# Order of the forward weave's steps, and of the work at the border behind it, in a fused attention forward and backward kernel

## The chip, the cores and the metric

The kernel runs on one core of a Trainium2 chip. The metric is the device time of one execution in microseconds (us); several executions are timed and their median is taken. The core has five engines: TensorE (PE; weight loads are shown as PEld), VectorE (DVE), ScalarE (ACT), GpSimd (POOL) and SyncE (SP, which issues DMA transfers). Each runs its own instructions in order and waits on semaphores for the others.

## The reference, cut to what matters

The reference computes two attention layers on the same 2048 tokens of width 576, mixes them with a gate, and takes all gradients.

```python
# A: 32 heads of width 18, one shared key and value (k = x @ wk, v = x @ wv)
scores = einsum('bhqd,bkd->bhqk', q, k) * 18 ** -0.5
a = merge(einsum('bhqk,bkd->bhqd', softmax(scores), v)) @ wo
# B: 32 heads of width 128, segments of 32 tokens, 8 memory rows carried from one to the next
for s in range(64):
    h = concat([mem, x[32 * s:32 * s + 32]])          # 40 rows
    q, k, v = (einsum('btd,dhe->bhte', h, W) for W in (Wq, Wk, Wv))
    p = softmax(where(mask, einsum('bhqe,bhke->bhqk', q, k) * 128 ** -0.5, -1e9))
    o = einsum('bhte,hed->btd', einsum('bhqk,bhke->bhqe', p, v), Wo)
    mem, out_s = o[:8], o[8:]
out = g * a + (1 - g) * b                              # g = sigmoid(x . gate_w)
# and the gradients of out with respect to x, every weight, mem0 and gate_w
```

Layer B's memory makes its segments a chain: segment s + 1 cannot begin before the eight memory rows of segment s are known. Layer A has no such chain.

## The kernel before, in words

The program runs in stages. First come transposes, weights and the projections of all tokens (to 420 us). Then the **forward weave** (420 to 2060): the forward chain of layer B's memory rows and the first sweep over layer A's pairs of query and key tiles, interleaved by hand. Then the **bulk** (2060 to 2660): layer B's attention and its gradients for all tokens of all segments at once. A second weave (2660 to 4335) joins the backward chain to a second sweep over layer A, and the weight gradients end the program.

**The weave.** `weave` (L277) advances two generators in turn, two sweep steps ahead: one part of the chain, then one step of the sweep. The order of the instructions on each engine is the order of these calls; no scheduler moves them.

- The chain, `b_chain_fwd` (L338), yields 16 times a segment, 64 segments. A sweep has 1024 steps, numbered n; the text calls n % 16 the **place**. The first part of a segment stands in front of place 2, the second in front of place 3, and so on.
- The parts that matter: part 1 (in front of place 2) takes `row_sums` (L306): four transposes of 32-bit values by PE into c_pj, summed by DVE into the new memory rows hm. Parts 2 to 4 project the keys: two halves ("k", 0) into c_pj and ("k", 1) into c_x, five contraction tiles each, four matmuls a tile (four column groups of the array, side by side). Before, parts 2, 3, 4 hold 2, 4 and 4 tiles (L461 to L472). Parts 5 to 7 project queries and the later ones values. In part 11 POOL normalises the probabilities (c_pn) and spreads them over heads by `expand` (L260): c_PBm for the memory rows, then c_PBx for the tokens (L520, L521). In part 13 (in front of place 14) PE multiplies tokens' values by c_PBx and then memory values by c_PBm (L531 to L535).
- The sweep, `a_pass1` (L1761): in step n, PE makes the scores a_S of tile n + 1 and a_dP of tile n; ACT takes the exp of a_S into a_E (L1778); DVE multiplies a_dP by a_E into a_W (L1811); PE then adds tile n - 1's a_E and a_W to a_acc. There is one a_S buffer. All 16 key tiles of a query block make one round of 16 steps; then ACT copies a_acc to a_acs (place 0) and a generator `a_post` (L1840) finishes the block in pieces: at place 3, ahead of the scores, two transposes of a_acs into c_x (the tile name that the chain's second key half also uses) and ACT's copy to a_tk; at place 10 two transposed loads of the queries a_qt; at place 14 two transposes into c_pj and DVE's copy to a_tk; at place 15 some fifteen small operations on POOL, with the results stored by SP.

**The border.** For the last query block all of `a_post` runs behind the last step, its small operations on DVE. Its a_qt takes a buffer of the a_W ring, so SP's two transposed loads wait until one is free; its a_tk is the one buffer that the block before it still reads on POOL. `b_bulk` (L664) then clears four block-diagonal tiles x_vmB and x_kmB on DVE (L669, L670, 128x1024 words each) and issues the loads of its first chunks on SP (L918 to L924). Every row of its loop over t runs a list of pipelined pieces, `order`, with their lags: t transposes queries and keys of group t (`trans`, L770, copied by DVE for q and k, by ACT for dO and v), takes scores and exp of group t - 1, and transposes dO and v of group t - 2. Four groups make a chunk. x_tr, which takes the transposes, has two buffers.

Which waits guard what is decided when the program is built: each instruction waits for the last reader or writer of the tile, or of the memory that a new tile takes over. Loads on SP also wait, in order, for the eighth load before them.

Of the kernel before, what the change touches and what calls it, by code (L numbers as in the profile page):

```python
# [12 lines left out]
BF16 = mybir.dt.bfloat16  # L13
F32 = mybir.dt.float32
U16 = mybir.dt.uint16
U32 = mybir.dt.uint32
P = 128

D = 576
# [27 lines left out]
class Kern:  # L47
# [290 lines left out]
    def b_chain_fwd(self, keep, sp, psum):  # L338
        nc = self.nc
        NSEG = self.NSEG  # L340
        hm = self.hm
        hx = keep.tile([P, 3, 64], F32, name="c_hx")
        PBm = keep.tile([P, 8, 64], BF16, name="c_PBm")
        nc.vector.memset(hx[:], 0.0)
# [63 lines left out]
        for s in range(NSEG):  # L408
# [49 lines left out]
            nc.gpsimd.tensor_copy(hist[:, :, s, :], h_[:, 0:NKT, 0:8])  # L458
            if not last:
                put_ride(s + 1)  # L460
            proj("k", 0, (0, 1))  # L461
            yield
            proj("k", 0, (2, 3, 4))
            proj("k", 1, (0,))
            if wt is not None:
                stash_end(*wt)
                wt = None
# [1 line left out]
                nc.gpsimd.dma_start(self.pq_dram[s // 4].rearrange("c i q s h x k -> (c i q) (s h x k)")  # L469
                                    .rearrange("p (n z) -> p n z", z=256), z4[:].unsqueeze(1).to_broadcast([P, 8, 256]))  # L470
            yield
            proj("k", 1, (1, 2, 3, 4))  # L472
            yield
            self.evac(flat(t2["k"], 1), pj["k", 1][:], use="s")
            proj("q", 0, (0, 1, 2, 3))
# [41 lines left out]
            pn = sp.tile([P, 2, 64], BF16, name="c_pn", bufs=1)  # L517
            nc.gpsimd.tensor_tensor(out=pn[:], in0=Et[:], in1=rd[:].unsqueeze(1).to_broadcast([P, 2, 64]), op=ALU.mult)
            PBx = sp.tile([P, 8, 4, 8], BF16, name="c_PBx", bufs=1)
            self.expand(PBm[:, :, 0:32].rearrange("p u (c q) -> p u c q", q=8), pn[:, 1].rearrange("p (u q) -> p u q", q=8), 8)  # L520
            self.expand(PBx[:], pn[:, 0].rearrange("p (u q) -> p u q", q=8), 8)  # L521
            nc.gpsimd.dma_start(self.pm_dram[s], pn[:].rearrange("p a b -> p (a b)"))
            proj("v", 1, (0, 1))
            yield
# [139 lines left out]
    def b_bulk(self, wp, vp, kp, sp, psum):  # L664
        nc = self.nc
        NTT = self.NTT
        mx = self.maskX
        mB = {w: [wp.tile([P, 4, 4, E], BF16, name=f"x_{w}mB{i}") for i in range(2)] for w in ("k", "v")}
        for t in mB["v"] + mB["k"]:  # L669
            nc.vector.memset(t[:], 0.0)  # L670
        mT = {}
        C = {}
        NG = NTT * 8
# [33 lines left out]
        deep = self.RING  # L707
# [62 lines left out]
        def trans(t, w, nb):  # L770
            tt, g, r, d = view(t)
            pt = psum.tile([P, 4, P], BF16, name="x_tr", bufs=2)
            for i in range(4):
                self.tr(pt[:, i, :], d[w][:, 4 * (g % 4) + i, :], P)
            o = sp.tile([P, 4, P], BF16, name=f"x_{w}T", bufs=nb)
            self.evac(o[:], pt[:], use="s" if w in ("dO", "v") else "v")
            sc[w + "T", t] = o

        st_QT = lambda t: trans(t, "q", 2)
# [135 lines left out]
                 (5, st_K), (3, st_D), (5, st_KE), (3, st_O), (5, st_Q)]  # L915
        after = {st_O: (("vB", 0), ("v", 0)), st_D: (("mT", 0),), st_KE: (("q", 0), ("dO", 1)), st_Q: (("kB", 0), ("k", 3))}
        later = {}
        load(0, ("q", "k", "mT", "dO"))  # L918
        load(1, deep)
        load(0, ("v", "vB", "kB"))  # L920
        load(1, ("v", "vB", "kB"))
        load(2, deep + ("mT", "v"))
        for c in range(3, BQ):
            load(c, deep)  # L924
        for t in range(NG + 6):
            if t == NG - 8:
                self.sweep_first()
            sc["D"] = psum.tile([P, 512], F32, name="x_D", bufs=1)
            sc["Sb"] = psum.tile([P, 512], F32, name="x_S", bufs=1)
            for n, st in order:  # L930
                if n is None:
                    st(t)
                    continue
                if 0 <= t - n < NG:
                    st(t - n)
                if st in after and t - n >= 0 and (t - n) % 4 == 3:
                    c = (t - n) // 4
                    for w, wait in after[st]:
                        later.setdefault(t + wait, []).append((c + (BQ if w in deep else 3 if w in ("mT", "v") else 2), (w,)))
                        if wait == 0:  # L940
                            load(*later[t].pop())
            if t % 4 == 2 and t // 4 - 2 in range(NTT // 4):
                self.dl_rows(t // 4 - 2, sp, psum)
            for x in later.pop(t, ()):
                load(*x)
            flush(t >= NG)
# [814 lines left out]
    def a_pass1(self, keep, sp, psum, xps):  # L1761
        nc = self.nc
        T, NTT = self.T, self.NTT
        NB = NPR * (T // 512)
        dl_all = self.dl_all
        S, E_, W_ = {}, {}, {}
        QD, load = self.QD, self.load_QD

        def mm_S(n):
            S[n] = psum.tile([P, 2, 512], F32, name="a_S", bufs=1)  # L1770
            kt = n % 16
            for i in range(2):
                r = slice(32 * i, 32 * i + 32)
                self.mm(S[n][:, i, :], lhsT=self.KV[r, kt * P:kt * P + P], rhs=QD[n // 16][r, :], tp=(32 * i, 0))

        def ex(n):
            E_[n] = sp.tile([P, 2, 512], BF16, name="a_E", bufs=3)
            nc.scalar.activation(E_[n][:], S.pop(n)[:], ACT.Exp, scale=SCALEA)  # L1778

        def acc_mm(acc, n, src, st, halves, first, last):  # L1780
            t = src.pop(n)
            for h in halves:
                for g in range(4):
                    self.mm(acc[32 * g:32 * g + 32, 256 * h:256 * h + 256],
                            lhsT=st[:, n % 16, 32 * h:32 * h + 32],
                            rhs=t[:, g % 2, 256 * (g // 2):256 * (g // 2) + 256],
                            start=first and h == 0, stop=last, tp=(0, 32 * g))

        mm_S(0)
        ex(0)  # L1790
        NP_ = 16 * NB
        acc = None
        post = None
        for n in range(NP_ + 1):
            if n < NP_:
                kt = n % 16
                if kt == 11:
                    load(n // 16 + 2)
                if post is not None and kt in (3, 14):
                    next(post)  # L1800
                if n + 1 < NP_:
                    mm_S(n + 1)
                dP = [psum.tile([P, 512], F32, name="a_dP", bufs=3) for _ in range(2)]
                for i in range(2):
                    r = slice(64 + 32 * i, 96 + 32 * i)
                    self.mm(dP[i][:], lhsT=self.KV[r, kt * P:kt * P + P], rhs=QD[n // 16][r, :], tp=(64 + 32 * i, 0))
                if n + 1 < NP_:
                    ex(n + 1)
                W_[n] = sp.tile([P, 2, 512], BF16, name="a_W", bufs=2)
                for i in range(2):  # L1810
                    nc.vector.tensor_tensor(out=W_[n][:, i, :], in0=dP[i][:], in1=E_[n][:, i, :], op=ALU.mult)  # L1811
            if n > 0:
                if n % 16 == 1:
                    acc = psum.tile([P, 512], F32, name="a_acc", bufs=1)
# [12 lines left out]
        for _ in post:  # L1827
            pass
# [11 lines left out]
    def a_post(self, b, acs, sp, psum, dl_all):  # L1840
# [4 lines left out]
        eng = nc.vector if end else nc.gpsimd  # L1845

        def queries():
            qt = sp.tile([P, 2, 2, P], BF16, name="a_qt", tag="a_W" if end else "a_qt", bufs=2 if end else 1)
            src = self.qs_blk(b, 0)
            for a in range(2):  # L1850
                nc.sync.dma_start_transpose(qt[:, a], src[a])
            return qt

        def half(hf):
            pt = psum.tile([P, 2, P], F32, name=("c_x", "c_pj")[hf], bufs=1)
            for j in range(2):
                nc.tensor.transpose(pt[:, j, :], acs[:, (2 * hf + j) * P:(2 * hf + j + 1) * P], self.identF[:])
            self.evac(tk[:, :, :, 32 * hf:32 * hf + 32], pt[:].rearrange("p t (g c) -> p t g c", c=32), use="sv"[hf])

        if end:  # L1860
            qt = queries()
        tk = sp.tile([P, 2, 4, 64], F32, name="a_tk", bufs=1)
        half(0)
        yield
        if not end:
            qt = queries()
        yield
        half(1)
        yield
        rl = sp.tile([P, 2, 2, 4], F32, name="a_rl", bufs=2)  # L1870
        nc.vector.reciprocal(rl[:, 1], tk[:, :, :, 18])
# [23 lines left out]
        r4 = sp.tile([P, 2, 2, 2, 2], F32, name="a_r4", bufs=2)  # L1895
        for w in range(2):
            eng.tensor_copy(r4[:, :, :, w, :], rl[:, w].rearrange("p t (a i) -> p a t i", i=2))
        q4 = qt[:].rearrange("p a t (b c) -> p (a t b) c", c=32)
        eng.tensor_tensor(out=q4, in0=q4, op=ALU.mult,
                                in1=r4[:].rearrange("p a t w i -> p (a t w i)").unsqueeze(2).to_broadcast([P, 16, 32]))  # L1900
        dq_.dma_start(self.qs_blk(b, 1).rearrange("a p c -> p a c"), qt[:].rearrange("p a t x -> p a (t x)"))

    def sweep_first(self):
        self.QS = [self.wr.tile([P, 2, 512], BF16, name=f"b_QS{c}", bufs=1) for c in range(2)]
# [350 lines left out]
```

## Time and profile before

| what | us |
|---|---|
| median of 3 runs | 5364.2 (5357.48 to 5371.53) |
| the profiled execution's own time | 5351.38 |
| its span, first to last instruction | 5349.7 |
| forward weave (420 to 2060) | 1640 |
| bulk (2060 to 2660) | 600 |
| second weave (2660 to 4335) | 1675 |
| granted TensorE clock, mean | 0.984 |

A row of a timeline gives start and duration in us, the engine, the line of the kernel, the operation, "out<-in" by tile names, the shape and type, how many instructions are merged (x2), and in brackets how long the engine had been idle and what ended that. "issue" stands where nothing that the profile shows ended it. SPq is SP issuing a DMA; such a row lasts as long as SP is held. A row of a tile's answer gives counts and minimum, median and maximum duration in nanoseconds, with the first and last start in us. Durations of matmuls are modelled and overlap: starts are what counts. The chain of waits goes back from the last instruction, at each step to what released it.

### The profile page before, as it was taken

Reading aid. Unit: us, or ns where it says so; the run is one execution under the profiler, and the core shown is the slowest. Engines: PE = TensorE matmul, PEld = TensorE weight load, DVE = VectorE, ACT = ScalarE, POOL = GpSimd, SP = SyncE. Lnnn points to the kernel's source line nnn. Section 1 sums busy time; section 2 is a strip of 40 time slices with the busy share of each in tenths; the row PEclk is TensorE's granted clock in tenths of the full one; section 3 lists DMA queues with packets and bytes.
Section 4 is the critical chain, followed back from the end, with each engine's and each line's share of the span. In section 5 each row is a group of like instructions: output and inputs, shape, how many; then the busy total and the mean of one; then the engine's idle time right before and its main releaser. Section 6 shows DMA issues by size and latency. Waiting matters only on the chain.

```text
span 5349.7 us, 218056 instructions
## 1 busy us (share of the span) xinstructions
PE 5023.2 (94%) x93298; PEld 2941.2 (55%) x93476; DVE 3619.4 (68%) x7146; ACT 3323.5 (62%) x4816; POOL 2421.1 (45%) x4634
## 2 busy tenths in 40 slices
PE   7999999999999998988879999999999999999999
PEld 5434555555555555777735555555554467764444
DVE  5337888888888887777778888888888831111112
ACT  4327888888888886666668888888887732111101
POOL 4004555555555554444436666666654321222223
PEclk9999999999999999999989999999999999999999
DMA  6655655665665445878866889888876679976653
GB/s 217 227 182 131 146 140 143 140 144 144 140 143 131 119 107 181 247 235 241 242 202 170 193 196 199 199 197 200 196 172 140 148 165 224 265 229 210 195 175 114
DMA packets 1115775, 961.45 MB, mean 180 GB/s; under 512 B 690738, under 2 KB 942139, under 8 KB 1105202
## 3 DMA queue, kind: packets, MB, share of 16 engines
q1 hardware_dynamic: 1013730, 702.18, 53.2%
q0 software_dynamic: 100928, 245.16, 15.2%
q8 instruction: 731, 11.98, 1.0%
q14 instruction: 242, 1.98, 0.1%
q10 hardware_dynamic: 144, 0.15, 0.0%
HBM read 521.16 MB, written 357.96 MB: 164 GB/s over the span
## 4 chain that ended last, share of the span: by engine, by line
PE 72%; ACT 9%; issue 9%; POOL 3%; DMA 2%; DVE 1%; SPq 1%; POOLq 0%; ACTq 0%; DVEq 0%
PE w_acc L82 12%; PE r_pj L82 7%; PE b_S L82 6%; PE a_S L82 6%; PE a_acc L82 5%; PE c_pj L82 5%; ACT b_E L1951 5%; PE b_acc L82 5%; PE r_x L82 5%; PE p_pb L82 4%; PE c_x L82 4%; ACT a_E L1778 4%; PE x_tr L87 3%; PE x_b L82 2%; PE x_po L82 2%
## 5 line engine op out<-in xcount | busy, mean ns | idle before, releaser
L1974 DVE TENSOR_TENSOR b_dS<-b_dP,b_E 128x512 bf16<-128x512 f32 x2048 | 1314.3, 683 | 224.7 <-issue 91.1
L1811 DVE TENSOR_TENSOR a_W<-a_dP,a_E 128x512 bf16<-128x512 f32 x2048 | 1313.0, 683 | 206.7 <-issue 76.8
L1951 ACT ACTIVATE b_E<-b_S 128x1024 bf16<-128x1024 f32 x1024 | 1048.8, 1024 | 285.4 <-PE b_dP L82 196.2
L1778 ACT ACTIVATE a_E<-a_S 128x1024 bf16<-128x1024 f32 x1024 | 1049.9, 1025 | 240.0 <-PE a_dP L82 192.7
L82 PEld LDWEIGHTS <-b_QS 32*128 32x128 bf16 (+1 forms) x8192 | 270.3, 92 | 522.8 <-issue 463.5
L82 PE MATMUL r_pj<-WT,r_dT 128*32 128x288 bf16 x12288 | 497.2, 287 | 6.0 <-issue 6.0
L82 PE MATMUL b_S<-b_KV,b_QS 32*128 32x512 bf16 x2048 | 405.1, 383 | 92.7 <-ACT b_E L1951 60.8
L82 PE MATMUL w_acc<-w_d,w_h 128*128 128x512 bf16 (+1 forms) x2352 | 470.9, 379 | 2.5
L82 PE MATMUL a_S<-a_QD,l_KV 32*128 32x512 bf16 x2048 | 399.6, 381 | 42.6 <-ACT a_E L1778 20.5
L82 PE MATMUL b_acc<-b_dS,b_QS 128*32 128x512 bf16 x2048 | 424.4, 393 | 0.2
L82 PE MATMUL a_acc<-a_E,l_VK 128*32 128x256 bf16 x8192 | 412.2, 278 | 5.0
L82 PE MATMUL b_acc<-b_E,b_QS 128*32 128x512 bf16 x2048 | 407.1, 394 | 0.0
L82 PE MATMUL b_dP<-b_KV,b_QS 32*128 32x512 bf16 x2048 | 403.8, 389 | 0.1
L82 PE MATMUL a_dP<-a_QD,l_KV 32*128 32x512 bf16 x2048 | 398.6, 385 | 0.1
L82 PEld LDWEIGHTS <-r_dT 128*32 128x32 bf16 x12288 | 336.4, 97 | 97.6 <-issue 10.6
L82 PEld LDWEIGHTS <-w_h 128*128 128x128 bf16 (+1 forms) x2688 | 230.0, 100 | 258.2 <-issue 6.6
L82 PEld LDWEIGHTS <-l_KV 32*128 32x128 bf16 x4096 | 150.1, 91 | 288.1 <-issue 264.4
L82 PE MATMUL a_acc<-a_W,l_WK 128*32 128x256 bf16 x4096 | 291.3, 273 | 0.4 <-DVE a_W L1811 0.3
L79 ACT CAST w_o<-w_acc 128x512 bf16<-128x512 f32 x54 | 31.6, 586 | 384.2 <-PE w_acc L82 358.7
L77 DVE CAST w_o<-w_acc 128x512 bf16<-128x512 f32 x54 | 37.4, 692 | 335.1 <-PE w_acc L82 307.2
L82 PEld LDWEIGHTS <-l_VK 128*32 128x32 bf16 x8192 | 128.9, 94 | 236.9 <-issue 233.1
L1092 POOL TENSOR_TENSOR r_kb<-r_ks,bmask 128x512 bf16<-128x512 bf16 x176 | 188.7, 1072 | 105.2 <-DMA r_ks<-px_dram 39.8
(482 smaller groups left out, 10609.6 us busy)
## 6 DMA issues: line engine op xcount, KB each, us to landing
b_QS<-qs_dram SPq DMA_DIRECT2D x256, 256.0 KB
dOx_dram<-p_tok SPq DMA_DIRECT2D x16, 1024.0 KB
c_vx<-vx_dram SPq DMA_DIRECT2D x64, 256.0 KB
krow_dram<-c_k POOLq DMA_DIRECT2D x64, 256.0 KB, 3.5
qrow_dram<-c_q POOLq DMA_DIRECT2D x64, 256.0 KB, 4.3
vrow_dram<-c_v POOLq DMA_DIRECT2D x64, 256.0 KB, 6.5
x_q<-qx_dram SPq DMA_DIRECT2D x32, 512.0 KB
x_k<-kx_dram SPq DMA_DIRECT2D x32, 512.0 KB
```

The costliest lines, as they stand in the source:

```text
L77: nc.vector.tensor_copy(out, in_)
L79: nc.scalar.copy(out, in_)
L82: return self.nc.tensor.matmul(out, lhsT, rhs, start=start, stop=stop, tile_position=tp, skip_group_check=True)
L87: return self.nc.tensor.transpose(out, in_, self.identB[b:b + nrows, b:b + nrows], tile_position=tp)
L1092: nc.gpsimd.tensor_tensor(out=B[:], in0=a[:].unsqueeze(2).to_broadcast([P, 4, 4, SEG]), in1=self.bmask[:, :, 0].unsqueeze(1).unsqueeze(3). ...
L1778: nc.scalar.activation(E_[n][:], S.pop(n)[:], ACT.Exp, scale=SCALEA)
L1811: nc.vector.tensor_tensor(out=W_[n][:, i, :], in0=dP[i][:], in1=E_[n][:, i, :], op=ALU.mult)
L1951: nc.scalar.activation(E_[n][:], S.pop(n)[:], ACT.Exp, scale=SCALEA)
L1974: nc.vector.tensor_tensor(out=D_[n][:, i, :], in0=dP[i][:], in1=E_[n][:, i, :], op=ALU.mult)
```

## The change

Four places are edited; the computation stays the same.

1. In part 11 the spread of the token probabilities (c_PBx) is issued ahead of that of the memory rows (c_PBm).
2. Key projection: parts 2, 3, 4 hold 3, 4, 3 contraction tiles in place of 2, 4, 4.
3. The first two transposes of `a_post` move from place 3 to place 2 (still ahead of the scores), and ACT's copy of them is issued behind that place's exp. The later pieces of `a_post` keep their places.
4. The border: the last block's queries are loaded into a c_wt buffer of the chain from place 11 of the last round (n = 1019) on, its a_tk takes a buffer of the a_E ring, the bulk clears one masked tile at the end of each of its first four steps with that tile's load behind it, the first chunk's v is loaded ahead of the second chunk, the loads of later chunks follow in steps 0 to 2, and step 0's copies of q and k run on ACT.

```diff
+        self.cfs = sp
...
-            proj("k", 0, (0, 1))
-            yield
-            proj("k", 0, (2, 3, 4))
-            proj("k", 1, (0,))
+            proj("k", 0, (0, 1, 2))
+            yield
+            proj("k", 0, (3, 4))
+            proj("k", 1, (0, 1))
...
-            proj("k", 1, (1, 2, 3, 4))
+            proj("k", 1, (2, 3, 4))
...
+            self.expand(PBx[:], pn[:, 0].rearrange("p (u q) -> p u q", q=8), 8)
             self.expand(PBm[:, :, 0:32].rearrange("p u (c q) -> p u c q", q=8), pn[:, 1].rearrange("p (u q) -> p u q", q=8), 8)
-            self.expand(PBx[:], pn[:, 0].rearrange("p (u q) -> p u q", q=8), 8)
...
-        for t in mB["v"] + mB["k"]:
-            nc.vector.memset(t[:], 0.0)
...
-            self.evac(o[:], pt[:], use="s" if w in ("dO", "v") else "v")
+            self.evac(o[:], pt[:], use="s" if w in ("dO", "v") or t == 0 else "v")
...
-        load(0, ("q", "k", "mT", "dO"))
+        load(0, ("q", "k", "mT", "dO", "v"))
         load(1, deep)
-        load(0, ("v", "vB", "kB"))
-        load(1, ("v", "vB", "kB"))
-        load(2, deep + ("mT", "v"))
-        for c in range(3, BQ):
-            load(c, deep)
+
+        def first(t):
+            if t < 4:
+                nc.vector.memset(mB["vk"[t // 2]][t % 2][:], 0.0)
+                load(t % 2, ("vk"[t // 2] + "B",))
+            if t == 0:
+                load(1, ("v",))
+            elif t == 1:
+                load(2, deep)
+            elif t == 2:
+                load(2, ("mT", "v"))
+                for c in range(3, BQ):
+                    load(c, deep)
...
+            first(t)
             if t % 4 == 2 and t // 4 - 2 in range(NTT // 4):
...
-                if post is not None and kt in (3, 14):
+                for _ in range((kt == 2) + 2 * (kt == 14) if post is not None else 0):
                     next(post)
+                if n == NP_ - 5:
+                    self.qt_last = self.cfs.tile([P, D], BF16, name="c_wt", bufs=2)[:, 0:512].rearrange(
+                        "p (a t x) -> p a t x", a=2, t=2)
+                    for a, src in enumerate(self.qs_blk(NB - 1, 0)):
+                        nc.sync.dma_start_transpose(self.qt_last[:, a], src)
                 if n + 1 < NP_:
                     mm_S(n + 1)
...
                     ex(n + 1)
+                if post is not None and kt == 2:
+                    next(post)
...
         def half(hf):
...
+            return pt
+
+        def half_out(hf, pt):
             self.evac(tk[:, :, :, 32 * hf:32 * hf + 32], pt[:].rearrange("p t (g c) -> p t g c", c=32), use="sv"[hf])

         if end:
-            qt = queries()
-        tk = sp.tile([P, 2, 4, 64], F32, name="a_tk", bufs=1)
-        half(0)
+            qt = self.qt_last
+        tk = sp.tile([P, 2, 4, 64], F32, name="a_tk", tag="a_E" if end else "a_tk", bufs=3 if end else 1)
+        pt = half(0)
+        yield
+        half_out(0, pt)
         yield
         if not end:
             qt = queries()
         yield
-        half(1)
+        pt = half(1)
+        yield
+        half_out(1, pt)
         yield
```

More of the change, by code (lines that the diff above doesn't have):

```diff
@@ L1847, in queries @@
         def queries():
-            qt = sp.tile([P, 2, 2, P], BF16, name="a_qt", tag="a_W" if end else "a_qt", bufs=2 if end else 1)
+            qt = sp.tile([P, 2, 2, P], BF16, name="a_qt", bufs=1)
             src = self.qs_blk(b, 0)
@@ L1897, in a_post @@
             eng.tensor_copy(r4[:, :, :, w, :], rl[:, w].rearrange("p t (a i) -> p a t i", i=2))
-        q4 = qt[:].rearrange("p a t (b c) -> p (a t b) c", c=32)
+        qt = qt if end else qt[:]
+        q4 = qt.rearrange("p a t (b c) -> p (a t b) c", c=32)
         eng.tensor_tensor(out=q4, in0=q4, op=ALU.mult,
                                 in1=r4[:].rearrange("p a t w i -> p (a t w i)").unsqueeze(2).to_broadcast([P, 16, 32]))
-        dq_.dma_start(self.qs_blk(b, 1).rearrange("a p c -> p a c"), qt[:].rearrange("p a t x -> p a (t x)"))
+        dq_.dma_start(self.qs_blk(b, 1).rearrange("a p c -> p a c"), qt.rearrange("p a t x -> p a (t x)"))
     def sweep_first(self):
```

## The prediction

> **What bounds the kernel now.** I read the page first for the span, then the busy time by stage, then the first sweep's rows by engine over one segment (16 places, 25.5 us), and last the border behind it.
>
> ```profile
> span 5349.7 us, 218056 instructions
> ```
> ```profile
> 420.00:2060.00 1640.00, 1576.15 (x35124) 859.73 (x35124) 1419.71 (x2558) 1358.84 (x1792) 907.07 (x2089) 1.00 0.56 134
> 2060.00:2660.00 600.00, 521.32 (x14061) 432.56 (x14153) 437.27 (x1434) 363.12 (x774) 264.06 (x411) 0.96 0.81 242
> ```
>
> The columns are length, then PE, PEld, DVE, ACT and POOL busy, clock, DMA share and GB/s. The edits lie in the first row (the forward weave) and at the start of the second (the bulk). PE's 96% of the weave does not tell what bounds it: matmuls overlap. The exps of the first sweep tell it.
>
> ```profile
> L1778 ACT ACTIVATE a_E<-a_S x1024: 1024/1024/1043, 421.3 to 2058.0; 128x1024 bf16<-128x1024 f32 x171
> ```
> ```profile
> 1007.81 1.02 ACT L1778 ACTIVATE a_E<-a_S 128x1024 bf16<-128x1024 f32 x1
> 1009.03 0.37 ACT L537 CAST c_oT<-c_x 128x256 bf16<-128x256 f32 x1 [0.20 <-PE c_x L82]
> 1009.66 1.02 ACT L1778 ACTIVATE a_E<-a_S 128x1024 bf16<-128x1024 f32 x1 [0.25 <-PE a_dP L82]
> ...
> 1014.31 1.02 ACT L1778 ACTIVATE a_E<-a_S 128x1024 bf16<-128x1024 f32 x1
> 1015.86 1.02 ACT L1778 ACTIVATE a_E<-a_S 128x1024 bf16<-128x1024 f32 x1 [0.53 <-PE a_dP L82]
> 1017.14 0.37 ACT L79 COPY a_tk<-c_x 128x256 f32<-128x256 f32 x1 [0.25 <-PE c_x L1857]
> 1017.46 1.02 ACT L1778 ACTIVATE a_E<-a_S 128x1024 bf16<-128x1024 f32 x1
> ```
>
> There is one a_S buffer: the next scores wait for the exp to finish, and the next exp waits for the scores. This ring takes 1.02 us of exp, 0.05 to the scores and 0.48 from them: 1.55 us, the gap 1014.31 to 1015.86. No place can be shorter. The 1023 gaps in the grouped row take 1636.7 us, 51.1 more than 1.55 each. Sorted by place, the excess is: place 14 (1007.81 to 1009.66, 1.85 us) 18.9; places 3 to 7 4.3, 5.5, 5.4, 5.4 and 5.1; the other ten 6.5 together. At these places PE has more between two scores than the ring leaves it. Only that excess can be won, and any place filled beyond the ring adds to it.
>
> **The change part by part.**
>
> *Token probabilities first (place 14).*
>
> ```profile
> 1007.13 0.63 POOL L261 TENSOR_TENSOR c_PBm<-c_pn,bmask 128x256 bf16<-128x256 bf16 x1
> 1007.72 0.63 POOL L261 TENSOR_TENSOR c_PBx<-c_pn,bmask 128x256 bf16<-128x256 bf16 x1
> ```
> ```profile
> 1008.40 0.35 PE L82 MATMUL c_x<-c_PBx,c_vx 128*128 128x32 bf16 x8 [0.23 <-POOL c_PBx L261]
> 1008.60 0.39 PE L82 MATMUL c_x<-c_PBm,c_v 128*128 128x64 bf16 x8
> ...
> 1015.38 0.39 PE L82 MATMUL a_S<-a_QD,l_KV 32*128 32x512 bf16 x2
> ...
> 1016.06 0.61 PE L82 MATMUL c_pj<-Wk,hm 128*32 128x512 bf16 x8
> ```
>
> PE multiplies by c_PBx first, but POOL spreads it second, so PE stands from about 1008.10 to 1008.40, 0.05 after 1008.35. With the order turned, c_PBx is there at 1007.76, its eight matmuls run at 1008.10 to 1008.30, and the c_PBm ones start at 1008.40, when the second spread is done, in place of 1008.60. That is 0.20 us a segment and no more: 64 x 0.20 = **12.8 us**. What is late next is that second spread. The place stays at 1.65, above the ring, so nothing of it is hidden.
>
> *Keys 3, 4, 3 and the transposes one place sooner.* Counted in contraction tiles of four matmuls, places 3, 4, 5 (the parts behind places 2, 3, 4) held 2, 4, 4 and now hold 3, 4, 3. Eight matmuls last 0.61 us with 0.39 for one, so four cost 0.22. Place 3 had eight from 1016.06 and then two transposes; with twelve and no transposes the scores can go at 1016.06 + 0.55 + 0.22 = 1016.83, before the ring's 1015.38 + 1.55 = 1016.93. Place 3 falls to the ring: **-4.0**. Place 5 drops from sixteen to twelve by the same sum: **-5.0**, leaving both the 0.4 that undisturbed places show. Place 4 keeps sixteen and its excess.
>
> Place 2 receives the transposes, behind four others.
>
> ```profile
> 1014.75 0.20 PEld L310 LDWEIGHTS c_pj<-identF,c_hs 128*128 128x128 f32 x2 [0.21 <-issue]
> 1014.92 0.25 PEld L312 LDWEIGHTS c_pj<-identF,c_hx 128*128 128x128 f32 x2
> 1015.33 0.15 PEld L82 LDWEIGHTS <-l_KV 32*128 32x128 bf16 x4 [0.17 <-issue]
> ...
> 1016.61 0.20 PEld L1857 LDWEIGHTS c_x<-identF,a_acs 128*128 128x128 f32 x2 [0.42 <-issue]
> 1016.97 0.10 PEld L82 LDWEIGHTS <-l_KV 32*128 32x128 bf16 x4 [0.17 <-issue]
> ```
>
> Four transposes hold PE from 1014.75 to the scores' weights at 1015.33 (0.58); two alone take 1016.61 to 1016.97 (0.36). So two more in the same run cost 0.58 - 0.36 = 0.22. The scores started at 1015.38, so PE had 0.05 to spare: +0.17 a segment, 63 x 0.17 = **+10.7**. From the other side: the dear price of a run of its own is 0.36 - 0.05 = 0.31, +19.5. I take 0.17, since the new transposes follow four of their own kind. The copy to a_tk (0.37) goes behind place 2's exp: ACT stands idle 0.53 between two exps of the bare ring (row 1015.86), so it costs nothing; it would if it took over 0.53. It ends about 1 us before the keys' second half wants c_x. Weave: -12.8 - 4.0 - 5.0 + 10.7 = **-11.1 us**.
>
> *The border.*
>
> ```profile
> 2043.16 19.05 SPq L1851 DMA_TRANSPOSE a_qt<-qs_dram  x4
> ```
> ```profile
> 2060.97 1.25 SPq L1851
> ...
> 2067.25 14.21 DMA x_v<-vx_dram
> 2081.50 0.62 PE x_tr L87 x4
> ```
> ```profile
> 2055.33 0.39 PE L82 MATMUL c_pj<-Wvt,hm 128*32 128x512 bf16 x4
> ```
> ```profile
> 2064.76 0.42 DVE L77 COPY a_tk<-c_pj 128x256 f32<-128x256 f32 x1 [4.08 <-POOL a_t L1891]
> ...
> 2066.90 1.15 DVE L1890 TENSOR_TENSOR a_t<-a_tk,a_d 128x144 f32<-128x144 f32 x1
> 2068.09 0.31 DVE L1891 TENSOR_TENSOR a_t<-a_tk,a_t 128x144 f32<-128x144 f32 x1
> ...
> 2069.81 0.91 DVE L670 MEMSET x_vmB<- 128x1024 uint32 x1 [0.16 <-issue]
> ```
>
> SP's four transposed loads last to 2062.21 because the last block's two want an a_W buffer (the chain of waits has their tail, 1.25 us); then come nine loads in file, and the value rows, ninth at 2067.25 (0.63 each), land at 2081.50. Now the two transposes follow the earlier pair without a wait (an estimate of 2 us each, from that tail, lets all four end near 2052), the bulk's loads stand directly behind them, and in the program's order they wait only for the last use of the weights whose room they take (the value weights' row, to 2055.7); the values go sixth, right after the load that waits longest, near 2056.4. Even with the same 14.2 us of flight they land by 2070.6. The wait moves to DVE. The end block's copy no longer waits for POOL, because its tile is a free exp buffer: transposes end at 2062.3, so DVE runs 2.46 us sooner and reaches its first memset at 2067.35. One memset with its 0.16 gap is 1.07: 2068.4. Step 0's two copies now run on idle ACT. Step 1's two copies (0.42 each) reach 2069.3, the second memset 2070.3, a mask of 0.29 and step 2's two copies 2071.5; then the value transposes that stood at 2081.50 can go: 10.0 sooner. Two more memsets stand in the next two steps on DVE, 2 x 1.07 = 2.1, so I put **-8.0** (10.0 if both hide, 6 if DVE and POOL disturb each other more). The three memsets moved behind step 0 also hold SP, since each is followed by its masked load in order, with the next chunks' loads behind; the chunk needed first lies in front of them.
>
> [...]
>
> **Sum:** -11.1 - 8.0 = -19.1 us. The profiled execution's own time is 5351.4 (span 5349.7 and 1.7 around it): 5332.3. The median of the three runs, 5364.2, lies 12.8 above it, and all three (5357 to 5372) are above; a result will be such runs, so I add the 12.8: **5345.1**.
>
> **The rivals.**
>
> *Place 2 pays the dear price.* The six transposes cost as in a run of their own: +19.5 in place of +10.7, sum -10.3, 5353.9. For it: place 2 is at the ring's edge already. Against: in the rows the second pair of four costs less.
>
> *The bulk takes the border back.* Its DMA engines are at 0.81; the earlier start is met again by a later load. Then the weave's -11.1 alone: 5353.1. Against: loads start 10 us sooner too.
>
> *The spread order does nothing*, because PE's wait is really for both: -19.1 + 12.8 = -6.3, 5357.9. Against: the two groups of matmuls wait apart in the changed program's order.
>
> *More at the border:* with loads ahead, the next chunk's stalls go too. Place for it is some 9 us (a second wait like those 10): -28, 5336.
>
> *Slower.* PE's waits in the bulk that no engine ends:
>
> ```profile
> PE x_po L82 <- issue: 17.8, 14, 3.2
> PE x_D L82 <- issue: 16.7, 17, 3.1
> ```
>
> [...] If the thicker loads make them grow, the kernel gets slower from the point where they more than double: by 19.1 it is even, by 35.2 it is slower by 0.3%; at 2.2 times (+41.4) 5386.5. Against: only some 20 us of the 600 get thicker. [...]
>
> **How the numbers follow.** A measurement of this kernel tells about 0.3% (16 us) from no change. Forecast 0.58 (its own range 5336 to 5355), of which 0.40 is under 5348.1 and so faster, 0.18 within; more at the border 0.12, faster; dear place 2 0.10, bulk takes back 0.08, spread order idle 0.04, all within; slower 0.08. So faster 0.52, same 0.40, slower 0.08. The range goes from 5331 (below the fourth rival, with the runs' own scatter) to 5362 (above the third).
>
> **What would show it.** Exps of one segment after the change: place 14 1.65, places 3 and 5 1.55, place 2 1.72 (1.86 by the dear price), places 4, 6, 7 still 1.63; the sweep 1625.6 long from its first exp to its last. At the border: first bulk load issued before the sweep's last exp, no PE wait for value rows, first bulk exp about 10 us sooner against the sweep's end, the fourth still about 8 sooner. The prediction is wrong if place 2 goes beyond 1.75, if place 14 stays at 1.85, or if the bulk from its fourth exp to its last is longer by over 5 us.

## The result and the profile after

Medians of 20 executions each: 5365.4 us before (5343.4 to 5380.4), **5350.3 us after** (5331.7 to 5375.8). The ratio is 0.9973, 95% interval 0.9962 to 0.9984: 15 us shorter, 9 to 20 by the interval, where 19.1 had been forecast (to 5345.1, 5.2 under what came). The mark that the prediction set for a time that can be told from no change, 0.3%, lies inside the interval.

The profiled execution of after took 5362.9 us, among the longest of its 20, so whole spans can't be compared. Its stages can. The page of after, then the exps of the first sweep (a_E) and of the bulk (x_E), grouped: duration of one, first start to last:

```profile
span 5361.2 us, 218175 instructions
```
```profile
L1787 ACT ACTIVATE a_E<-a_S x1024: 1023/1023/1046, 421.9 to 2049.4; 128x1024 bf16<-128x1024 f32 x171
```
```profile
L800 ACT ACTIVATE x_E<-x_S x128: 383/390/403, 2058.8 to 2659.2; 128x256 bf16<-128x256 f32 x128
```

and the bulk's exps of the kernel before:

```profile
L801 ACT ACTIVATE x_E<-x_S x128: 384/389/402, 2075.7 to 2656.1; 128x256 bf16<-128x256 f32 x128
```

The sweep takes 1627.5 us (1636.7 before), and the bulk begins 9.4 us behind it (17.6 before). One segment on ACT after the change:

```profile
1055.99 1.02 ACT L1787 ACTIVATE a_E<-a_S 128x1024 bf16<-128x1024 f32 x1
...
1057.63 1.02 ACT L1787 ACTIVATE a_E<-a_S 128x1024 bf16<-128x1024 f32 x1 [0.25 <-PE a_dP L82]
...
1062.29 1.02 ACT L1787 ACTIVATE a_E<-a_S 128x1024 bf16<-128x1024 f32 x1
1064.01 1.02 ACT L1787 ACTIVATE a_E<-a_S 128x1024 bf16<-128x1024 f32 x1 [0.70 <-PE a_dP L82]
1064.93 0.37 ACT L79 COPY a_tk<-c_x 128x256 f32<-128x256 f32 x1
1065.56 1.02 ACT L1787 ACTIVATE a_E<-a_S 128x1024 bf16<-128x1024 f32 x1 [0.26 <-ACT a_tk L79]
```

Place 14 is the gap from 1055.99 to 1057.63, 1.64 in place of 1.85. Place 2 is 1062.29 to 1064.01, 1.72, where the ring alone gives 1.55. Place 3, the last gap, is at the ring, and the moved copy of 0.37 lies hidden in it. What place 14 waits for now is the second spread: POOL ends it at 1056.53, and PE takes it 0.05 later.

```profile
1055.90 0.63 POOL L261 TENSOR_TENSOR c_PBm<-c_pn,bmask 128x256 bf16<-128x256 bf16 x1
```
```profile
1056.58 0.39 PE L82 MATMUL c_x<-c_PBm,c_v 128*128 128x64 bf16 x8
```

Over all 64 segments, in excess over 1.55 each, after against before: place 14 6.2 against 18.9, place 2 11.4 against 0.6, place 3 1.4 against 4.3, place 5 0.4 against 5.4; the other twelve together are 0.6 more. The sum is -9.2. (Six profiles, this one among them, have the same weave; their sweeps take 1626.4 to 1630.0, so a single one is good to about 2 us.)

At the border, SP's first load of the bulk now stands 8.9 us ahead of the sweep's last exp, and PE waits for no value rows. What PE waits for there instead (the waits from 2035 to 2083), POOL's file from the last segment's stores to the bulk's first x_P, and DVE's four fills:

```profile
2040.52 0.53 SPq L703 DMA_DIRECT2D x_q<-qx_dram  x1
```
```profile
PE x_tr L87 <- DVE x_qT L77: 5.6, 3, 3.3
PE x_S L87 <- POOL x_P L816: 3.0, 1, 3.0
PE a_acc L82 <- issue: 1.7, 1, 1.7
PE x_po L82 <- DMA x_kmB<-km_dram: 1.6, 1, 1.6
```
```profile
2063.14 1.69 POOL L552 DMA_DIRECT2D oh_dram<-c_oh  x1
2064.72 0.69 POOL L424 DMA_DIRECT2D vm_dram<-vrow_dram  x1
2065.30 0.68 POOL L568 DMA_DIRECT2D memT_dram<-memT_hist  x1
...
2067.32 0.79 POOL L1925 DMA_DIRECT2D qs_dram<-c_wt  x1
2068.07 0.69 POOL L816 TENSOR_TENSOR x_P<-x_E,x_r 128x256 bf16<-128x256 bf16 x1
```
```profile
2060.79 0.91 DVE L922 MEMSET x_vmB<- 128x1024 uint32 x1 [0.16 <-issue]
...
2062.47 0.91 DVE L922 MEMSET x_vmB<- 128x1024 uint32 x1 [0.16 <-issue]
...
2064.55 0.18 DVE L814 RECIPROCAL x_r<-x_l 128x4 f32<-128x4 f32 x1
2064.89 0.91 DVE L922 MEMSET x_kmB<- 128x1024 uint32 x1 [0.16 <-issue]
...
2072.53 0.91 DVE L922 MEMSET x_kmB<- 128x1024 uint32 x1 [0.16 <-issue]
```

x_P's last input, the reciprocal, is there at 2064.73, but POOL issues stores until 2068.07, and PE stands 3.0 us. The a_acc row lies at the sweep's end, ahead of the first bulk exp: a wait that no engine ends, 1.7 us here and in e11, 1.1 or less in the other profiles.

The exps' starts in the profile of each kernel below, in us. The border is cut in two: from the sweep's last exp to the bulk's first, and from there to its fourth.

| kernel | sweep | to 1st bulk exp | 1st to 4th | 4th to last | second weave |
|---|---|---|---|---|---|
| before | 1636.8 | 17.6 | 13.6 | 566.8 | 1645.0 |
| e2, weave alone | 1629.0 | 17.6 | 12.8 | 587.2 | 1652.2 |
| e3, spread order alone | 1626.1 | 17.6 | 13.3 | 575.4 | 1646.0 |
| after | 1627.5 | 9.4 | 17.0 | 583.4 | 1657.2 |
| e1, border alone | 1635.7 | 6.6 | 18.0 | 579.1 | 1645.5 |
| e5, spread order and border | 1624.6 | 7.2 | 17.2 | 580.7 | 1647.4 |
| e4, transposes at place 11 | 1657.0 | 6.3 | 18.0 | 572.5 | 1643.3 |
| e6, spread ahead of the reciprocal | 1622.4 | 6.3 | 18.6 | 578.4 | 1652.6 |
| e7, stores on ACT | 1630.0 | 14.5 | 13.6 | 581.6 | 1648.2 |
| e8, stores and fills on ACT | 1627.0 | 15.3 | 10.5 | 581.3 | 1650.1 |
| e9, stores early | 1627.9 | 8.2 | 15.1 | 576.7 | 1649.7 |
| e10, fills on ACT | 1626.4 | 7.7 | 16.5 | 577.7 | 1649.4 |
| e11, all | 1620.6 | 10.0 | 13.6 | 568.2 | 1655.8 |

The last two columns hold nearly the same instructions in every row and still scatter by 20 and 14 us. The first three columns decide. Part of the scatter goes with the granted clock: from the fourth exp to the last it was 0.98 in before (566.8) and 0.97 in after (583.4). Over the whole profile it was 0.984 or 0.985 in before, e3 and e9 (566.8 to 576.7) and 0.981 to 0.983 in e1, e2 and e5 (579.1 to 587.2), but 0.985 in e7 (581.6) and 0.983 in e11 (568.2). In the 33 executions of the kernel before that stand beside e1 to e4, a clock lower by 0.001 goes with some 5 us more. Whether the clock is the cause is not shown. Where several of each are on record, the mean clocks of a kernel's executions and of those of before beside it differ by 0.001 at most, so some 5 us of a difference could be the clock's.

### The profile page after: what moved, and what is told of

It reads as the page before. It is cut to its first block, busy times and chain, and to the rows that moved or that the text cites. A ratio compares the mean times of both kernels' runs of the same rounds, so it can differ in the third digit from the quotient of the medians.

```text
span 5361.2 us, 218175 instructions
## 1 busy us (share of the span) xinstructions
PE 5037.3 (94%) x93476; PEld 2961.0 (55%) x93476; DVE 3622.6 (68%) x7144; ACT 3312.5 (62%) x4818; POOL 2419.5 (45%) x4634
## 4 chain that ended last, share of the span: by engine, by line
PE 73%; ACT 12%; issue 8%; DMA 2%; POOL 1%; DVE 0%; SPq 0%; POOLq 0%; ACTq 0%; DVEq 0%
PE w_acc L82 12%; ACT a_E L1787 7%; PE r_pj L82 7%; PE a_S L82 7%; PE b_S L82 6%; PE a_acc L82 5%; ACT b_E L1975 5%; PE b_acc L82 5%; PE c_pj L82 5%; PE p_pb L82 5%; PE r_x L82 5%; PE c_x L82 3%; PE x_tr L87 3%; PE x_b L82 2%; PE x_po L82 2%
## 5 line engine op out<-in xcount | busy, mean ns | idle before, releaser
L82 PE MATMUL a_S<-a_QD,l_KV 32*128 32x512 bf16 x2048 | 399.6, 381 | 51.0 <-ACT a_E L1787 20.4
```

The source lines that it names most:

```text
L82: return self.nc.tensor.matmul(out, lhsT, rhs, start=start, stop=stop, tile_position=tp, skip_group_check=True)
```

## Experiments: the parts alone

**Theory:** weave and border add up, and what after's profile loses behind the bulk's fourth exp is scatter. **Rival:** the bulk takes the earlier start back. e1 keeps the border edits and puts the weave back; e2 is the kernel before with the weave edits; e3 is the kernel before with the two spreads exchanged.

```diff
e1, against after:
-            self.expand(PBx[:], ...)
             self.expand(PBm[:, :, 0:32]...)
+            self.expand(PBx[:], ...)
-            proj("k", 0, (0, 1, 2))
+            proj("k", 0, (0, 1))
...
-                for _ in range((kt == 2) + 2 * (kt == 14) if post is not None else 0):
+                for _ in range(2 * (kt == 3) + 2 * (kt == 14) if post is not None else 0):
...
-                if post is not None and kt == 2:
-                    next(post)
e3, against before:
-            self.expand(PBm[:, :, 0:32]...)
             self.expand(PBx[:], ...)
+            self.expand(PBm[:, :, 0:32]...)
```

> The border edits alone, the weave as in the kernel before. Theory (the border is worth its 5 to 8 us and the bulk's longer course in the one profile of after was chance): sweep from first to last exp 1636.8 as before; last sweep exp to first bulk exp near 9.4 us (before 17.65); bulk from its fourth exp to its last 560 to 575; time 5 to 8 us under the kernel before, ratio 0.9985 to 0.9991. Rival (the bulk takes it back): the same 9.4, but the bulk from fourth exp to last again 580 or more (before 566.8), and the time no shorter than before, ratio 1.000 to 1.002.

> The weave edits alone (spread order, keys 3, 4, 3, first transposes at place 2 with their copy behind the exp), the border as before. Theory (the two halves of the change add up): sweep 1627.5, border 17.6, fourth bulk exp to last near 567, time about 9 us under the kernel before, ratio 0.9983. Rival (a faster sweep runs the border's loads into something): border over 20 us, ratio 0.999 or more.

> Only the order of the two spreads turned, all else as before. Theory (PE stood for the second spread, 0.20 us a segment): place 14 1.647 in place of 1.845, all other places as before, sweep 1624.1, time 12.8 us under the kernel before, ratio 0.9976. Rival (place 14 gained from the keys and transposes moved elsewhere): place 14 stays above 1.75, sweep 1630 or more.

Grouped exps of the sweep in e1, e2 and e3:

```profile
L1787 ACT ACTIVATE a_E<-a_S x1024: 1023/1023/1046, 420.4 to 2056.1; 128x1024 bf16<-128x1024 f32 x171
```
```profile
L1778 ACT ACTIVATE a_E<-a_S x1024: 1023/1023/1046, 417.8 to 2046.8; 128x1024 bf16<-128x1024 f32 x171
```
```profile
L1778 ACT ACTIVATE a_E<-a_S x1024: 1023/1023/1046, 420.7 to 2046.8; 128x1024 bf16<-128x1024 f32 x171
```

The sweeps are 1635.7, 1629.0 and 1626.1 us. Against the same runs of the kernel before (median 5363.3): e1 5352.2, ratio 0.9983 (0.997 to 0.9996); e2 5346.7, 0.9973 (0.996 to 0.9987); e3 5347.0, 0.997 (0.9958 to 0.9981). Border, weave and the exchange of two lines each make the kernel shorter alone, and the exchange brings as much as can be told of the whole change. By times the border and the weave add to more than the whole (by the ratios 9 and 14 us against 15, with intervals of 2 to 16, 7 to 21 and 9 to 20); that they add up is shown by the stages only. In e3 place 14 fell to 1.65, and none of the others moved by over 1.3 us in the sum of 64.

The rival is not borne out. The five profiles with the new border (after, e1, e4, e5, e6) reach the bulk's fourth exp 5.9 us sooner against the sweep's end than the three with the old one, the eighth 5.5, the sixteenth 6.1 and the 32nd 8.2 us sooner: the next loads do not take the start back. Behind that the scatter grows too wide to tell (3.6 sooner at the last exp, where the three old ones spread by 20). Behind the fourth exp the three profiles with the old border take 566.8, 587.2 and 575.4 (mean 576.5), the five with the new one 572.5 to 583.4 (mean 578.8). Neither e1 (579.1, where 560 to 575 had been expected) nor e2 (587.2, near 567) came as expected: the profile of before was simply the shortest of all rows. A loss of some us in the bulk's later part can't be excluded; that not all is given back, e1's time says.

## Experiments: places of the weave

e4 moves the first two transposes from place 2 to the idle time that PE shows at place 11, into spare columns of the c_x tile that holds the token scores; their copy is issued at place 12, ahead of its scores.

```diff
-            px = psum.tile([P, 192], F32, name="c_x", bufs=1)
+            px = psum.tile([P, 448], F32, name="c_x", bufs=1)
+            self.px = px
...
-                for _ in range((kt == 2) + 2 * (kt == 14) if post is not None else 0):
+                for _ in range((kt == 12) + 2 * (kt == 14) if post is not None else 0):
...
+                pt = self.px[:, 192:448]...
...
+        if not end:
+            qt = queries()
         pt = half(0)
         yield
         half_out(0, pt)
-        yield
-        if not end:
-            qt = queries()
```

> The kernel after, with the first two transposes moved from place 2 to the end of step 10 (place 11), into spare columns of the token scores' own c_x tile, and their copy a part later. Theory (a place pays only for what it holds beyond the ring: at place 11 PE stood 0.26 us idle ahead of the scores plus 0.07 of overlap that the full places show, against 0.31 for two transposes alone): place 2 falls from 1.728 to 1.56, place 11 stays under 1.60, sweep 1627.5 - 10.7 = 1616.8 (up to 1620), time some 10 us under after and 25 under before, ratio 0.9953. Rival (two transposes cost their price wherever they stand): place 11 rises by 0.17 to 0.31, sweep 1627 to 1636, ratio as after (0.997) or worse.

The time was 5372.2, ratio 1.0015 (1.0002 to 1.0028): slower than before. Place 2 fell to the ring, as expected, but place 11 rose to 1.76 and place 12 to 2.10. ACT in e4, from the exp that opens place 11 to the one that closes place 12, then PE's transposes and the row behind them:

```profile
1214.87 1.02 ACT L1788 ACTIVATE a_E<-a_S 128x1024 bf16<-128x1024 f32 x1 [0.53 <-PE a_dP L82]
...
1216.63 1.03 ACT L1788 ACTIVATE a_E<-a_S 128x1024 bf16<-128x1024 f32 x1
1218.46 0.37 ACT L79 COPY a_tk<-c_x 128x256 f32<-128x256 f32 x1 [0.80 <-DVE c_rd L518]
1218.73 1.03 ACT L1788 ACTIVATE a_E<-a_S 128x1024 bf16<-128x1024 f32 x1
```
```profile
1215.16 0.44 PE L1875 MATMUL c_x<-identF,a_acs 128*128 128x128 f32 x2
1215.53 0.40 PE L82 MATMUL c_pj<-Wvt,hm 128*32 128x512 bf16 x4
```

Two mistakes. The two transposes hold PE for 0.37, and only 0.16 of it was covered at place 11 (0.21 x 64 = 13.5 us, more than place 2's 10.8). Which part of the idle time could not be used stays open. And the copy, which reads the tile that DVE's reciprocal reads, waits for that reciprocal and stands in ACT's file ahead of the next exp. ACT waits 0.80 and starts that exp 0.27 after the copy; the ring leaves it 0.53 idle, so 0.55 a segment are added: place 12's excess is 35.1 us, against 2.2 in after. One more reading: with 0.5 us more ahead of it in each segment, place 14 went to 1.55. So what is left there should be a wait for POOL. e6 tests that: the masks are multiplied in while POOL waits for the reciprocal.

```diff
+            self.expand(PBx[:], Et[:, 0]...)          # behind c_E's exp
+            self.expand(PBm[:, :, 0:32]..., Et[:, 1]...)
...
-            nc.gpsimd.tensor_tensor(out=pn[:], in0=Et[:], in1=rd...)
-            self.expand(PBx[:], pn[:, 0]...)
-            self.expand(PBm[:, :, 0:32]..., pn[:, 1]...)
+            for pb in (PBx[:], PBm[:, :, 0:32]...):
+                nc.gpsimd.tensor_tensor(out=pb, in0=pb, in1=r4, op=ALU.mult)
+            nc.gpsimd.tensor_tensor(out=pn[:], in0=Et[:], in1=rd...)
```

e5 is after with keys and transposes put back (the lines of e1 without the exchange of the spreads).

> The kernel after with keys and first transposes put back (2, 4, 4, place 3): spread order and border are left. Theory (places add up: -4.0 and -5.0 at places 3 and 5 against +10.7 at place 2): places 2, 3 and 5 as in the kernel before (1.56, 1.60, 1.63), place 14 1.65, sweep 1626, 1 to 2 us shorter than after's 1627.5; time equal to after within what can be told, ratio 0.996 to 0.997. Rival (the keys' new deal also relieves later places): sweep 1630 or more.

> The kernel after, with both spreads made from the unnormalised exps while POOL waits for the reciprocal, and the reciprocal multiplied in afterwards, the product for the store last: 0.42 us of POOL leave the chain ahead of c_PBx and c_PBm, the results are the same numbers. Theory (place 14 still stands at 1.65 because PE waits for the second spread): place 14 falls to 1.55, sweep 1627.5 - 6 = 1621.5, the other places as in after; ratio 0.996. Rival (the two transposes at place 14 hold it, not POOL): place 14 stays at 1.65, or the two more POOL operations make other places longer, sweep 1627 or more.

Grouped exps of the sweep in e5 and in e6, and POOL's file in e6:

```profile
L1787 ACT ACTIVATE a_E<-a_S x1024: 1024/1024/1043, 420.0 to 2044.6; 128x1024 bf16<-128x1024 f32 x171
```
```profile
L1790 ACT ACTIVATE a_E<-a_S x1024: 1024/1024/1044, 420.7 to 2043.1; 128x1024 bf16<-128x1024 f32 x171
```
```profile
1050.14 0.62 POOL L261 TENSOR_TENSOR c_PBx<-c_E,bmask 128x256 bf16<-128x256 bf16 x1
1050.73 0.62 POOL L261 TENSOR_TENSOR c_PBm<-c_E,bmask 128x256 bf16<-128x256 bf16 x1
1051.40 0.68 POOL L524 TENSOR_TENSOR c_PBx<-c_PBx,c_rd 128x256 bf16<-128x256 bf16 x1
1052.04 0.67 POOL L524 TENSOR_TENSOR c_PBm<-c_PBm,c_rd 128x256 bf16<-128x256 bf16 x1
1052.67 0.43 POOL L525 TENSOR_TENSOR c_pn<-c_E,c_rd 128x128 bf16<-128x128 bf16 x1
```

e5's sweep is 1624.6, shorter than after's 1627.5: keys and transposes as changed cost some 3 us (2.6 as a mean of six profiles with them and two without; the prediction's own terms, -4.0 - 5.0 + 10.7, give +1.7). e5 5339.2, ratio 0.9953 (0.9939 to 0.9967). In e6 place 14 is 1.57 and the sweep 1622.4, 5 us off; 5344.8, 0.9956 (0.9933 to 0.9979). Both theories held by stage; e5's ratio came out better than the 0.996 to 0.997 expected, within its interval.

## Experiments: behind the border

From the sweep's end to the bulk's fourth exp the old border takes 30.8 us (mean of three), the new one 24.9 (mean of the five above): 5.9 won, not 8.0. The first exp comes 10.4 sooner (7.2 against 17.6), and 4.5 of that are lost again in the next three steps (17.8 against 13.2): 0.7 from the first to the second exp, 2.8 to the third (5.84 us in each of the five, 3.06 in each of the three), 1.0 to the fourth. PE's 3.0 us for x_P stand in the second of these steps in all five. **Theory:** POOL's file of stores holds x_P. **Rival:** DVE's fills. e7 gives two stores to ACT, e8 the fills too; e9 leaves memT_dram to POOL, but early; e10 moves the fills alone.

```diff
e7 and e8 (e9: oh_dram so, memT_dram on POOL behind the copy to hist):
-                nc.gpsimd.dma_start(self.oh_dram...)
+                (nc.scalar if last else nc.gpsimd).dma_start(self.oh_dram...)
-                nc.gpsimd.dma_start(self.memT_dram[:], hist[:])
+                nc.scalar.dma_start(self.memT_dram[:], hist[:])
e8 and e10:
-                nc.vector.memset(mB["vk"[t // 2]][t % 2][:], 0.0)
+                nc.scalar.copy(mB["vk"[t // 2]][t % 2][:]..., self.zeros[:]...)
```

> The kernel after, with the last segment's two stores (oh_dram 1.69 us of issue, memT_dram 0.68) issued by ACT in place of POOL. Theory (behind the first bulk exp POOL's file of store issues holds x_P, and PE waits 3.0 us for it): POOL reaches its first x_P some 2.4 us sooner against the first bulk exp, PE's wait for x_P shrinks from 3.0 to under 1, first to fourth bulk exp 15 to 16 us (17.0, 18.0 and 18.0 in the three profiles with this border so far); time some 2 us less, too little to tell. Rival (DVE's memsets are what is late): first to fourth stays at 17 to 18, x_P only waits for its reciprocal.

> As the kernel with the two stores on ACT, and the four zero fills of the mask tiles too made by ACT (a copy of zeros) in place of DVE. Theory (DVE pays 1.07 us for each fill in steps 0 to 3, POOL's file apart): second bulk exp about 1 us sooner than with the stores alone, first to fourth 13 to 15 us, as short as before the change (12.8 to 13.6) but 10 us sooner against the sweep's end. Rival (ACT's fills of some 2 us each hold the copies to x_dOT and x_vT): first to fourth 17 us or more.

e7: 5352.8, 0.9972 (0.9959 to 0.9984); e8: 5346.2, 0.9975 (0.9961 to 0.9988): as after. In both ACT was held by something nobody had asked about; ACT and its queue in e7:

```profile
2051.17 8.16 ACTq L568 DMA_DIRECT2D memT_dram<-memT_hist  x1
2059.45 0.37 ACT L79 COPY a_tk<-c_x 128x256 f32<-128x256 f32 x1 [7.70 <-issue]
```

The bulk's first exp came 7 us late, so e7's clean 13.6 behind it proves little: everything else had been late too. e8's further 3.1 (10.5) is the fills' share, at that. Hence the next two.

> The kernel after, with POOL's file behind the last block made shorter without holding ACT: the memT_dram store (8.2 us of issue on ACT's queue in the earlier run, 0.68 on POOL's) goes out on POOL right after its last row is copied, fourteen parts earlier; the oh_dram store stays on ACT (0.64). Theory (POOL's file of store issues holds x_P, with nothing else wrong): last sweep exp to first bulk exp 6 to 9 us as in the other runs with this border, POOL's first x_P some 2 us sooner against it, PE's 3.0 us for x_P under 1.2, first to fourth bulk exp 15 to 16 us. Rival (in the earlier run x_P only looked prompt because all else was 7.7 us late): PE's wait for x_P stays near 3.0, first to fourth 17 to 18.

> The kernel after, with only the four zero fills moved from DVE to ACT (1.9 us each there). Theory (both POOL's file and DVE's fills are on the path): POOL's file still ends as late, so PE still waits 3 us or more for x_P in step 2; later steps lose their fills: first to fourth bulk exp 14.5 to 16.5 us. Rival (DVE's fills alone set the border): first to fourth 13.5 us or less, no wait for x_P over 1 us. Second rival (POOL's file alone): 17 us or more.

PE's waits at the border in e9 and in e10:

```profile
PE x_S L87 <- POOL x_P L816: 0.9, 1, 0.9
```
```profile
PE x_S L87 <- POOL x_P L816: 7.5, 2, 4.8
```

With a shorter file on POOL (e9) PE's wait for x_P falls from 3.0 to 0.9, the step from the second to the third exp from 5.84 to 3.95, and the first to the fourth from 17.8 to 15.1. That step took 5.84 in all five profiles before, so one profile is enough: POOL is shown. Without the fills on DVE (e10) the first to the fourth falls to 16.5 only: the first step is 2.3 us shorter, but PE then stands 4.8 us for the same POOL in the second. Both are on the path, POOL for the greater part. The rest of e10's 7.5, 2.7 us behind the fourth exp, is another wait: POOL stands until the store of memT_dram has landed, in after too, and no longer in e9.

```profile
2073.26 0.61 POOL L878 TENSOR_TENSOR x_Y<-x_P,x_dl 128x256 f32<-128x256 bf16 x1 [5.35 <-DMA memT_dram<-memT_hist]
```
```profile
2073.86 0.61 POOL L878 TENSOR_TENSOR x_Y<-x_P,x_dl 128x256 f32<-128x256 bf16 x1 [2.58 <-DMA memT_dram<-memT_hist]
```

So the early store shortens one wait and takes another away; what the other, behind the fourth exp, is worth alone no run tells. One execution each gave 5351.4 (e9) and 5340.7 (e10), which says nothing within this kernel's scatter.

Last, what the runs point to, together: e5, with e6's spreads, e9's stores and the fills on ACT.

> What the runs so far point to, together: the kernel after with keys and first transposes put back (2, 4, 4, place 3), both spreads made ahead of the reciprocal, the four fills on ACT, the last segment's oh_dram store on ACT and its memT_dram store sent early. Theory (the parts add up): sweep 1624.6 - 6 = 1618 to 1620, last sweep exp to first bulk exp 6 to 9 us, first to fourth 10.5 to 12, so the fourth bulk exp some 18 us behind the sweep's end (31 in the kernel before, 24 to 26 in after); time 25 to 31 us under the kernel before, ratio 0.9942 to 0.9953, and under after. Rival (the bulk gives the earlier start back): the same stages up to the fourth exp, but the bulk from there 590 or more and the ratio 0.996 or above.

```profile
L1791 ACT ACTIVATE a_E<-a_S x1024: 1024/1024/1043, 419.8 to 2040.4; 128x1024 bf16<-128x1024 f32 x171
```
```profile
PE x_S L87 <- POOL x_P L819: 2.6, 1, 2.6
```

e11: 5337.8 (12 executions), ratio 0.996 (0.9944 to 0.9977). The sweep, 1620.6, is the shortest of all rows, but the border is 23.6, not 18, and the ratio missed the 0.9942 to 0.9953 expected: the parts did not add up there. The first exp had the 1.7 us at the sweep's end ahead of it, and x_P still made PE wait 2.6: without the fills the second exp comes 4.3 us behind the first (6.7 in e9), and even POOL's shorter file is late against it. By stages e11 is 23 us under before; the time agrees (21). By the ratios it lies 7 us under after, e5 11; their intervals overlap after's, so neither is shown to beat it by time alone. By the first three columns both do, by 10 and 5 us, in one profile each.

## Why the prediction was right, and where it was short

- **Place 14, -12.8:** measured -12.7 in after and, alone in e3, -12.5. That the second spread is late next is shown by e6, which takes off 5 of the 6 us that were left.
- **Places 3 and 5, -4.0 and -5.0:** -3.0 and -5.1. Place 3's median is at the ring (1.551); one long gap of 2.6 us holds part of the rest.
- **Place 2, +10.7:** +10.8. The price of two transposes behind four was read rightly from two other rows. That a pair in a run of its own is dearer is shown by e4 (0.37).
- **Weave, -11.1:** -9.2 in after. Of the 1.9 missing, 1.0 is place 3's; the rest lies in the other places, mostly 12 (two long gaps) and 4 (0.005 more in most segments). Such long gaps move from run to run: e2 has one of 3.17 us at place 13, e3 one of 3.01 at place 4.
- **The border's first exp, 10.0 sooner:** 8.2 in after's profile, 10.4 as a mean of five (after's is the latest of them, with the 1.7 us at the sweep's end). The values come in time and the loads start ahead of the sweep's end, as said.
- **The border as a whole, -8.0: too large, 5.9 measured** (4.9 in after's own profile). The step that failed is "two more memsets stand in the next two steps on DVE", taken as the only thing that is late next. The last of them did cost its 1.0, between the third and the fourth exp. But the other lies beside POOL's file of stores, and that file holds the step from the second to the third exp for 2.8 us more; in the kernel before it was over 3.3 us before POOL's first x_P had its input. The step priced the wait that went and did not ask who else had been covered by it.
- **DVE beside POOL:** the 6 us named for the border if the two disturb each other more was the author's estimate; no run shows a price that adds up to it, and that it lies near the 5.9 is chance. The op that took 1.15 us in before while POOL made a product beside it (1.20) takes 0.31 in after, where POOL has just ended a product and goes on to a store. POOL's row in before, then DVE's in after:

```profile
2066.70 1.20 POOL L1899 TENSOR_TENSOR a_qt<-a_qt,a_r 128x512 bf16<-128x512 bf16 x1
```
```profile
2058.73 0.31 DVE L1913 TENSOR_TENSOR a_t<-a_tk,a_d 128x144 f32<-128x144 f32 x1 [0.32 <-POOL a_dq L1916]
```

So the 1.15 did not come back in after. POOL's product beside DVE's chain was the longer one, 1.38 against 1.04 (the rows at the end).

- **The slower rival** (PE's waits that no engine ends) did not come. In after's bulk they are 33.0 us, against 34.5. Counted over all rows of that kind, from the bulk's fourth exp to its last, they are 56.7 against 51.1, but 59.0 and 57.7 in e2 and e3 with the old border, so the new border is not what makes them. What stands behind these waits, and that thicker loads make them grow, no run shows.

```profile
PE x_D L82 <- issue: 19.8, 15, 3.3
PE x_po L82 <- issue: 13.2, 10, 3.0
```

- **"Wrong if the bulk from its fourth exp to its last is longer by over 5 us":** after's profile is longer there by 16.6, and so is e2's by 20.4, with the old border. The mark was set on one profile of before without knowing the scatter of that stretch; it can't judge.

Together -9.2 and -5.9 make -15.1; the medians differ by 15.1. That the two agree so closely is chance: the times allow 9 to 20, and the terms come from different profiles. The forecast's mechanism held in the weave and up to the border's second exp (9.8 us sooner), and its sum was 4 us too large. Its step from one profile to the median, 12.8 added, was needed: over 20 executions the profile of before lies 14.0 under its kernel's median, while after's lies 12.6 above.

## What to carry to other kernels

Where one ring sets the pace, sort its gaps by place and price each edit only by what its place holds beyond the ring; that sum held to 1 to 4 us in 1637 (1625.6 forecast, 1626.4 to 1630.0 in the six profiles of that weave). When a stall is removed at a border, list every engine's file up to that moment, stores included: each that ended inside the stall becomes the next candidate. And before a few us in a long stretch are read from one profile, look how that stretch scatters in kernels that don't touch it.

## What the runs showed of the hardware that was not expected

The same store of memT_dram occupied ACT's queue 8.16 us (8.52 in e8) and held the engine's next operation 7.70 us, where POOL issues it in 0.68 in after and in e9, fourteen parts earlier, in 0.56:

```profile
L463 POOL DMA_DIRECT2D memT_dram<-memT_hist x1: 558/558/558, 2032.5 to 2032.5; - x1
```

The oh_dram store went the other way: 0.64 on ACT, 1.69 on POOL. What makes the one long is not settled. ACT's hold in e7 also left DVE idle for 7.00 us while POOL made its product of 128x512: 1.04 us there (and in e8, with DVE idle for 6.92), 1.38 in after with DVE's chain beside it. DVE's own product of that size keeps its length, 0.69 in e7 and 0.71 in after. POOL's row in e7, then in after:

```profile
2056.90 1.04 POOL L1923 TENSOR_TENSOR a_qt<-a_qt,a_r 128x512 bf16<-128x512 bf16 x1
```
```profile
2060.16 1.38 POOL L1923 TENSOR_TENSOR a_qt<-a_qt,a_r 128x512 bf16<-128x512 bf16 x1
```
